# The second MLP's cosine with its argument in periods, its coefficients in two tiles, and a new order of instructions

## The chip, the cores and the metric

The kernel runs on one core of one Trainium2 chip. The metric is the device time of one execution in microseconds (us). The kernel before took 601.26 us, the median of three runs (601.25 to 602.89).

## The reference

The program computes an attention with a local window and block summaries, and behind it two MLPs on the same 1536 tokens of 512 features. Cut to what matters:

```python
# attention: 2 batches, 8 heads, 768 positions, 64 features a head
k_sum = k.reshape(B, H, nb, 32, D).max(axis=3)      # one maximum and one mean per block of 32
v_sum = v.reshape(B, H, nb, 32, D).mean(axis=3)
scores_l = scale * q @ k.T   # kept where |i - j| < 16
scores_s = scale * q @ k_sum.T + log(32)
a = softmax(concat([scores_l, scores_s]))
x = a @ concat([v, v_sum])
# first MLP: 512 -> 2048 -> 512
h = x @ w_in
g = (a0 + a1*h + a2*h**2 + a3*h**3) / (1 + abs(b0)*abs(h) + abs(b1)*h**2 + 1e-6)
x = g @ w_out
# second MLP, same sizes
h = x @ w_in
out = (h * cos(h)) @ w_out
```

All is in float32, except that the weights of both MLPs arrive as 8-byte floats.

## The kernel before

*Attention* is worked off in twelve units of 128 rows (six a batch). For the first batch, four pairs of heads are loaded as two k tiles each (line 454) and transposed on TensorE into a tile `ktp` (line 463); a copy (lines 322 and 327, by ScalarE or VectorE) puts them where the scores read them, and a reduction on VectorE (line 471) takes the maximum of the key blocks. The first unit's q rows come in two loads (line 559), are transposed into `qtp` (line 432) and copied to `qT`. Score products (line 626) go into `sp`; VectorE adds the mask and takes a row minimum (line 656), ScalarE takes the exponential, the normalised rows (line 673 multiplies) are transposed, and products with v (line 734, VectorE or GpSimd having added rows for the v means before) give the unit's output. The v means themselves are products with a selection matrix into `vmp` (line 542).

*The MLPs* take the tokens in three tiles T of 512 and the 2048 inner features in 16 tiles f of 128, four to a group. One pair of an f and a T is a unit; there are 48 a layer (the very first tile is cut in halves). A unit has its first product into `h` (line 864; in layer two from f = 2 on, two units share seven smaller products, line 962), its activation on ScalarE, VectorE and GpSimd, a split of the result into two parts `gh` and `gl` (lines 775 and 777), and the second product, which sums into four tiles `acc` (line 1106). Each product of 32-bit numbers is three TensorE products of such parts. The weights are put together from their 8-byte words by three VectorE instructions a tile (lines 760, 764, 768) and split in the same way. At the end of a group the `acc` tiles are copied out (line 1132), and put back (a copy again) when the token tile comes up next. When layer one has summed over all f, the copy is made by `x_keep` (line 893) and split for layer two; in layer two's last group the copies feed the output's DMAs, and the last of all are made by `mlp_end`.

*The activation of layer two* (`ew2`, lines 1045 to 1070) finds h·cos h. ScalarE turns h/2π into a whole number K (line 1057), VectorE takes K·2π from h in two steps, as 6.28125·K and the rest (line 1061, twice a unit), ScalarE takes the absolute value (line 1064) and then the sine of π/2 minus it (line 1066), and VectorE multiplies by h (line 1069).

*The coefficients* a and b come by two small loads into one tile `co`; three ScalarE and four VectorE instructions (lines 383 to 398) work out √|b1|, a scale that layer one's activation needs.

*The order.* The program first collects its operations (`P.op`), each with the engines that can do it, and then issues them in the order of a table, `ORDER`, which holds for each operation its place and the engine that does it. The times that stand with the operations are those by which the table was planned; with a table given they decide nothing. SyncE issues nearly all loads in its part of the same order. An engine works off its own part in order and waits where a tile that it needs isn't ready or isn't free.

## Time and profile before

| | |
|---|---|
| runs, median of 3 | 601.26 us |
| profiled execution, span | 599.4 us |
| TensorE busy (products) | 585.9 us, 98% |
| TensorE busy (weight loads, which run beside the products) | 501.0 us, 84% |
| VectorE busy | 548.4 us, 92% |
| ScalarE busy | 434.1 us, 72% |
| GpSimd busy | 304.3 us, 51% |
| granted TensorE clock | 9 in all 40 slices, which is 90% of full speed or more |

The profile is of one execution. The page gives its span, from its first to its last instruction, and no other time of that execution. In rows of the trace PE stands for TensorE, PEld for its weight loads, DVE for VectorE, ACT for ScalarE, POOL for GpSimd and SP for SyncE; L463 is line 463 of the kernel; `acc<-gh,w` says that `acc` is written from `gh` and `w`. The releaser named beside idle time is what ended it.

### The profile page before, as it was taken

Reading aid. Unit: us, or ns where it says so; the run is one execution under the profiler, and the core shown is the slowest. Engines: PE = TensorE matmul, PEld = TensorE weight load, DVE = VectorE, ACT = ScalarE, POOL = GpSimd, SP = SyncE. Lnnn points to the kernel's source line nnn. Section 1 sums busy time; section 2 is a strip of 40 time slices with the busy share of each in tenths; the row PEclk is TensorE's granted clock in tenths of the full one; section 3 lists DMA queues with packets and bytes.
Section 4 is the critical chain, followed back from the end, with each engine's and each line's share of the span. In section 5 each row is a group of like instructions: output and inputs, shape, how many; then the busy total and the mean of one; then the engine's idle time right before and its main releaser. Section 6 shows DMA issues by size and latency. Waiting matters only on the chain.

```text
span 599.4 us, 10933 instructions
## 1 busy us (share of the span) xinstructions
PE 585.9 (98%) x3897; PEld 501.0 (84%) x3897; DVE 548.4 (92%) x1119; ACT 434.1 (72%) x954; POOL 304.3 (51%) x303
## 2 busy tenths in 40 slices
PE   8879999999999999999999999999999999999997
PEld 7568878888888888888888888888989989998996
DVE  4999999979999999998999999999999998887874
ACT  3989999877587756876789897766767566554653
POOL 5587975247537564557577542444355423732130
PEclk9999999999999999999999999999999999999999
DMA  9897874200321313311220112123322331100104
GB/s 264 218 258 192 204 209 120 75 0 2 106 71 37 106 36 105 106 52 56 70 71 1 36 36 71 37 71 104 109 71 70 106 108 36 35 1 1 53 1 158
DMA packets 68862, 51.85 MB, mean 87 GB/s; under 512 B 37304, under 2 KB 63160, under 8 KB 68808
## 3 DMA queue, kind: packets, MB, share of 16 engines
q1 hardware_dynamic: 68664, 51.03, 29.0%
q8 instruction: 30, 0.49, 0.3%
q14 instruction: 24, 0.20, 0.1%
q10 hardware_dynamic: 144, 0.13, 0.1%
HBM read 47.71 MB, written 3.15 MB: 85 GB/s over the span
## 4 chain that ended last, share of the span: by engine, by line
PE 87%; DVE 9%; ACT 2%; DMA 1%; issue 0%; POOL 0%; SPq 0%; POOLq 0%; DVEq 0%; ACTq 0%
PE acc L1106 43%; PE h L864 22%; PE h L962 18%; DVE sc L656 2%; DMA vw<-in_v_dram 1%; PE avp L734 1%; DVE f L764 1%; DVE f L768 1%; PE ptp L687 1%; PE sp L626 1%; PE warm L356 1%; PE ktp L463 1%; DVE f L760 1%; PE vmp L542 0%; DVE big L471 0%
## 5 line engine op out<-in xcount | busy, mean ns | idle before, releaser
L1106 PE MATMUL acc<-gh,w 128*128 128x512 f32 (+1 forms) x416 | 123.1, 378 | 0.0
L1106 PE MATMUL acc<-w,gh 128*128 128x512 f32 x382 | 119.3, 394 | 0.0
L864 PE MATMUL h<-xH,w 128*128 128x512 f32 (+1 forms) x320 | 99.1, 371 | 0.1
L777 POOL TENSOR_TENSOR gl<-te,gh 128x512 fp32r<-128x512 f32 (+1 forms) x48 | 62.7, 1307 | 67.2 <-ACT gh L322 33.5
L1106 PEld LDWEIGHTS acc<-gh,w 128*128 128x128 f32 x416 | 75.3, 188 | 14.9 <-issue 1.5
L1106 PE MATMUL acc<-gl,w 128*128 128x512 f32 (+1 forms) x208 | 77.6, 373 | 0.0
L1106 PEld LDWEIGHTS acc<-w,gh 128*128 128x128 f32 x382 | 66.7, 189 | 9.4
L1106 PE MATMUL acc<-w,gl 128*128 128x512 f32 x191 | 74.3, 389 | 0.0
L1023 POOL TENSOR_TENSOR tu<-tu,tf 128x512 f32<-128x512 f32 (+1 forms) x41 | 51.4, 1255 | 41.2 <-ACT tf L1015 40.9
L777 POOL TENSOR_TENSOR w<-f,w 128x512 fp32r<-128x512 f32 x39 | 54.4, 1397 | 29.5 <-ACT w L322 15.0
L864 PEld LDWEIGHTS h<-xH,w 128*128 128x128 f32 x320 | 58.5, 188 | 10.6 <-DVE big L495 0.3
L864 PE MATMUL h<-xL,w 128*128 128x512 f32 (+1 forms) x160 | 58.9, 368 | 0.0
L864 PE MATMUL h<-big,w 128*128 128x512 f32 x216 | 52.0, 389 | 0.0
L768 DVE SCALAR_TENSOR_TENSOR f<-raw,f 128x512 int32<-128x512 int32 x64 | 48.3, 759 | 0.3
L1013 ACT ACTIVATE tu<-h,co 128x512 f32<-128x512 f32 (+1 forms) x52 | 33.9, 652 | 19.3 <-PE h L864 18.2
L764 DVE SCALAR_TENSOR_TENSOR f<-raw,f 128x512 int32<-128x512 int32 x64 | 47.3, 745 | 0.6
L864 PEld LDWEIGHTS h<-big,w 128*128 128x128 f32 x216 | 40.6, 188 | 8.4
L1106 PEld LDWEIGHTS acc<-gl,w 128*128 128x128 f32 x208 | 39.1, 188 | 7.0
L1106 PEld LDWEIGHTS acc<-w,gl 128*128 128x128 f32 x191 | 35.9, 188 | 7.9
L1057 ACT ACTIVATE tu<-te 128x512 int32<-128x512 f32 x27 | 17.1, 632 | 32.5 <-DVE te L987 32.2
L324 POOL TENSOR_SCALAR w<-f 128x512 fp32r<-128x512 f32 x28 | 20.0, 715 | 39.8 <-DVE f L768 35.1
L1033 ACT ACTIVATE h<-tf 128x512 f32<-128x512 f32 (+1 forms) x52 | 29.6, 570 | 12.0 <-DVE te L1027 10.8
(222 smaller groups left out, 1530.9 us busy)
## 6 DMA issues: line engine op xcount, KB each, us to landing
raw<-in_moe_w_in_dram SPq DMA_DIRECT2D x32, 512.0 KB, 4.6
raw<-in_moe_w_out_dram SPq DMA_DIRECT2D x32, 512.0 KB, 3.4
vw<-in_v_dram SPq DMA_DIRECT2D x24, 192.0 KB, 3.5
qk<-in_q_dram SPq DMA_DIRECT2D x10, 256.0 KB, 5.3
out_dram<-part SPq DMA_DIRECT2D x8, 256.0 KB, 2.8
part<-in_k_dram SPq DMA_DIRECT2D x8, 192.0 KB, 4.8
big<-in_v_dram SPq DMA_DIRECT2D x3, 512.0 KB, 6.7
qk<-in_k_dram SPq DMA_DIRECT2D x6, 256.0 KB, 5.4
```

The lines of the kernel that those rows point to most:

```text
L324: nc.gpsimd.tensor_scalar(out=o, in0=i, scalar1=1.0, scalar2=1.0, op0=ALU.mult, op1=ALU.mult)
L656: lambda e, pr=pr, hh=hh, sv=sv, sp=sp: nc.vector.tensor_tensor_reduce(out=sv()[:, pr, :], in0=sp.t[:, pr, :], in1=m.t, op0=ALU.add, op1=A ...
L764: lambda e: nc.vector.scalar_tensor_tensor(out=ft.t.bitcast(I32), in0=lohi()[1], scalar=-0x40000000, in1=ft.t.bitcast(I32), op0=ALU.bitwis ...
L768: lambda e: nc.vector.scalar_tensor_tensor(out=ft.t.bitcast(I32), in0=lohi()[0], scalar=29, in1=ft.t.bitcast(I32), op0=ALU.logical_shift_r ...
L777: lambda e: E[e].tensor_tensor(out=lo(), in0=x(), in1=hi().bitcast(F32), op=ALU.subtract),
L864: nc.tensor.matmul(out=h.t[:, 0:n], lhsT=lt, rhs=rt[:, kk, cs], start=(k0 == 0 and i == 0), stop=(k0 == 2 and i == 5))
L962: nc.tensor.matmul(out=bank.t[:, c], lhsT=lt, rhs=rt, start=start and i == 0, stop=stop and i == 5, skip_group_check=True)
L1013: lambda e: nc.scalar.activation(out=U(), in_=H(), func=ACTF.Square, scale=b1s))
L1023: lambda e: E[e].tensor_tensor(out=U(), in0=U(), in1=Z(), op=ALU.add))
L1033: lambda e: nc.scalar.activation(out=H(), in_=Z(), func=ACTF.Exp, scale=-1.0))
L1057: lambda e: nc.scalar.activation(out=K().bitcast(I32), in_=S_(), func=ACTF.Identity, scale=1.0 / (2.0 * math.pi)))
L1106: nc.tensor.matmul(out=dst, lhsT=lt, rhs=rt, start=(un.start and not have and i == 0), stop=(un.stop and i == 2), skip_group_check=have)
```

## The change

1. *The cosine.* From the output of layer one on, values are kept in a unit in which 0.875 (`PER`) is one period of the cosine: `x_keep` multiplies by 0.875/2π where it copied, and the output copies multiply by 2π/0.875. K is then h/0.875 + 0.25 as a whole number, and h − 0.875·K is one step, as 0.875·K needs few bits. The sine is taken of 2π/0.875 times this plus π/2, without an absolute value. Each of the 48 units of layer two loses one VectorE and one ScalarE instruction; 12 copies at the end of layer one and 13 at the output become scaled copies (`cps`).
2. *The coefficients.* a stays in `co`, b and what is made from it get a tile of their own, `cb`.
3. *The order.* The table is new (2944 operations instead of 3040). The planning times beside the operations are new too.

```diff
+PER = 0.875
+TURN = PER / (2.0 * math.pi)
 ORDER = (
-    "c-rk)ON?g6RsQOA-*w;jf4}<g{`)o4-P7Zq=^1+-9?wi>?7=wWB#vccTP8ROa%>aJ1|csTD`5dy#8QX>i%1qqK!CD{;t"
...
-MM = 0.2275
-SPT = 1.2
+MM = 0.2267
+SPT = 0.98
...
+    def cps(e, o, i, x):
+        if e == "A":
+            nc.scalar.activation(out=o, in_=i, func=ACTF.Identity, scale=x)
+        else:
+            nc.vector.tensor_scalar(out=o, in0=i, scalar1=x, scalar2=None, op0=ALU.mult)
...
-    co_r = fixed([128, 12], F32, "co")
-    co = co_r.t
+    co_r = fixed([128, 4], F32, "co")
+    cb_r = fixed([128, 5], F32, "cb")
+    co, cb = co_r.t, cb_r.t
...
-    b0, b1s = co[:, 4:5], co[:, 8:9]
+    b0, b1s = cb[:, 0:1], cb[:, 3:4]
...
-        P.op([("S", 0.1)], [], [co_r], lambda e: nc.sync.dma_start(out=co[:, 4:6], in_=moe_b.partition_broadcast(128)))
+        P.op([("S", 0.1)], [], [cb_r], lambda e: nc.sync.dma_start(out=cb[:, 0:2], in_=moe_b.partition_broadcast(128)))
-        P.op([("A", 0.2)], [], [co_r],
-             lambda e: nc.scalar.activation(out=co[:, 7:8], in_=co[:, 5:6], func=ACTF.Abs))
+        P.op([("A", 0.2)], [], [cb_r],
+             lambda e: nc.scalar.activation(out=cb[:, 2:3], in_=cb[:, 1:2], func=ACTF.Abs))
...
@@ x_keep
-        P.op([("A", act(512, True)), ("V", dve(512))], [ac], [rx[d]], lambda e: cp(e, x()[:, d], ac.t))
+        P.op([("A", act(512, True)), ("V", dve(512))], [ac], [rx[d]],
+             lambda e: cps(e, x()[:, d], ac.t, TURN))
@@ ew2
              lambda e: nc.scalar.activation(out=K().bitcast(I32), in_=S_(), func=ACTF.Identity,
-                                            scale=1.0 / (2.0 * math.pi)))
-        for c, x in ((C1, S_), (C2, H)):
-            P.op([("V", dve2(512) if x is S_ else dve(512))], [tu] + s2, hb,
-                 lambda e, c=c, x=x: nc.vector.scalar_tensor_tensor(
-                     out=H(), in0=K().bitcast(I32), scalar=-c, in1=x(), op0=ALU.mult, op1=ALU.add))
-        P.op([("A", act(512, True))], [], hb,
-             lambda e: nc.scalar.activation(out=H(), in_=H(), func=ACTF.Abs))
+                                            scale=1.0 / PER, bias=0.25))
+        P.op([("V", dve2(512) if un.s is not None else dve(512))], [tu] + s2, hb,
+             lambda e: nc.vector.scalar_tensor_tensor(
+                 out=H(), in0=K().bitcast(I32), scalar=-PER, in1=S_() if un.s is not None else H(),
+                 op0=ALU.mult, op1=ALU.add))
         P.op([("A", act(512, True))], [], hb + [table],
-             lambda e: nc.scalar.activation(out=H(), in_=H(), func=ACTF.Sin, scale=-1.0,
+             lambda e: nc.scalar.activation(out=H(), in_=H(), func=ACTF.Sin, scale=2.0 * math.pi / PER,
                                             bias=math.pi / 2))
@@ mlp_o
-                 lambda e, ac=ac, sl=sl: cp(e, sl(), ac.t))
+                 lambda e, ac=ac, sl=sl, last=un.last: (cps(e, sl(), ac.t, 1.0 / TURN) if last
+                                                        else cp(e, sl(), ac.t)))
@@ mlp_end
-            P.op([(e0, 0.3)], [ac], [res[x]], lambda e, c=c, sl=sl: cp(e, sl(), ac.t[:, c]))
+            P.op([(e0, 0.3)], [ac], [res[x]],
+                 lambda e, c=c, sl=sl: cps(e, sl(), ac.t[:, c], 1.0 / TURN))
```

What the new table moves is seen in the order in which each engine gets its instructions. Lines of the changed kernel stand six or seven further down than those of before. The first place is the opening of SyncE's queue, where `part` is the tile of the k and q loads, `big` that of v, and x2 says that a row stands for two instructions. Before:

```order
L454 DMA part<-in_k_dram 128x2x192 x2
L559 DMA part<-in_q_dram 128x4x128
L454 DMA part<-in_k_dram 128x2x192
L559 DMA part<-in_q_dram 128x4x128
L454 DMA part<-in_k_dram 128x2x192 x5
L507 DMA big<-in_v_dram 128x8x128 x3
```

After:

```order
L387 DMA cb<-in_moe_b_dram 128x2
L460 DMA part<-in_k_dram 128x2x192 x8
L565 DMA part<-in_q_dram 128x4x128 x2
L513 DMA big<-in_v_dram 128x8x128 x3
L421 DMA raw<-in_moe_w_in_dram 128x4x128
L421 DMA qk<-in_q_dram 128x8x64 x2
```

The load of b, which stood behind the opening, is first; the q loads, which stood between k loads, follow all eight of these.

The same opening on TensorE, where one k tile is six instructions of the `ktp` row, and one q load's transposition eight of the `qtp` row. Before:

```order
L356 MATMUL warm<-ident 128x128 x8
L463 MATMUL ktp<-ident,part 64x128 x12
L432 MATMUL qtp<-ident,part 64x64 x16
L463 MATMUL ktp<-ident,part 64x128 x30
L432 MATMUL qtp<-ident,part 64x64 x8
L626 MATMUL sp_290<-room,qT_214 64x120
L626 MATMUL sp_292<-room,qT_214 64x120
```

After:

```order
L362 MATMUL warm<-ident 128x128 x8
L469 MATMUL ktp<-ident,part 64x128 x48
L438 MATMUL qtp<-ident,part 64x64 x16
L632 MATMUL sp_303<-room,qT_290 64x120
L632 MATMUL sp_305<-room,qT_290 64x120
```

Two k tiles and both parts of the first q loads came ahead of five more k tiles and of the first score product; now all eight k tiles come first, then the q tiles.

The third place is VectorE's end, where the last two units of layer two are made (their h is in `h` and `te` or `tu`, `gl` is the low part that the last products read) and the last output copies stand (`room<-acc`). Before:

```order
L1061 SCALAR_TENSOR_TENSOR h<-tu,te 128x512
L1061 SCALAR_TENSOR_TENSOR h<-tu,h 128x512
L327 COPY acc_6848<-room 128x512
L327 COPY acc_6862<-room 128x512
L1069 TENSOR_TENSOR te<-te,h 128x512
L1061 SCALAR_TENSOR_TENSOR h<-tu 128x512
L327 CAST gh<-te 128x512
L1061 SCALAR_TENSOR_TENSOR h<-tu,h 128x512
L777 TENSOR_TENSOR gl<-te,gh 128x512
L1069 TENSOR_TENSOR tu<-tu,h 128x512
L327 CAST gh<-tu 128x512
L777 TENSOR_TENSOR gl<-tu,gh 128x512
```

After:

```order
L994 TENSOR_TENSOR te<-h,te 128x512
L332 COPY acc_6755<-room 128x512
L991 TENSOR_TENSOR tu<-h,tu 128x256
L1067 SCALAR_TENSOR_TENSOR h<-tu,te 128x512
L332 COPY tu<-h 128x256
L1074 TENSOR_TENSOR te<-te,h 128x512
L1067 SCALAR_TENSOR_TENSOR h<-tu 128x512
L783 TENSOR_TENSOR gl<-te,gh 128x512
L1074 TENSOR_TENSOR tu<-tu,h 128x512
L783 TENSOR_TENSOR gl<-tu,gh 128x512
```

One subtraction a unit is gone, and one copy back into `acc` stands between, where there were two. On TensorE 13 groups of three products stood between the last first-layer product and the first group that reads the last `gl`; now there are 8.

## Rows read from the trace of the kernel before

**Rows 1.** The head of the page: span, and busy time of each engine

```profile
span 599.4 us, 10933 instructions
...
PE 585.9 (98%) x3897; PEld 501.0 (84%) x3897; DVE 548.4 (92%) x1119; ACT 434.1 (72%) x954; POOL 304.3 (51%) x303
```

**Rows 2.** Busy us of PE, PEld, DVE, ACT, POOL; clock, DMA share, GB/s

```profile
0.00:20.00 20.00, 16.85 (x244) 13.66 (x244) 11.09 (x45) 9.28 (x35) 11.25 (x39) 1.00 0.94 262
20.00:40.00 20.00, 15.92 (x223) 12.07 (x222) 19.77 (x78) 19.33 (x75) 12.95 (x14) 1.00 0.87 218
40.00:60.00 20.00, 18.31 (x234) 16.43 (x235) 20.00 (x74) 18.97 (x67) 15.25 (x19) 1.00 0.81 219
...
420.00:440.00 20.00, 20.00 (x130) 18.16 (x129) 19.78 (x35) 15.08 (x32) 7.87 (x8) 1.00 0.41 127
```

**Rows 3.** TensorE in order of time: start, us, instruction, [idle before]

```profile
7.39 0.68 PE L432 MATMUL qtp<-ident,part 64*64 64x64 f32 x16
...
9.28 3.58 PE L463 MATMUL ktp<-ident,part 128*64 128x128 f32 x60
...
45.81 1.15 PE L734 MATMUL avp<-pt,vw 120*64 120x64 f32 x32
...
64.05 0.66 PE L489 MATMUL ktp<-ident,qk 128*128 128x128 f32 x4
...
73.53 1.02 PE L542 MATMUL vmp<-raw,vsel 128*24 128x512 f32 x2 [0.60 <-DVE mn L656]
...
94.77 1.44 PE L734 MATMUL avp<-pt,vw 120*64 120x64 f32 x32
...
591.96 0.62 PE L1106 MATMUL acc<-w,gh 128*128 128x512 f32 x2
```

**Rows 4.** The chain that ended last: start, us, what

```profile
14.71 1.44 DVE big L514
...
63.01 0.40 DVE te L1027
...
87.47 7.66 DMA vw<-in_v_dram
```

**Rows 5.** SyncE's queue in order of time, opening and end

```profile
0.81 0.94 SPq L454 DMA_DIRECT2D part<-in_k_dram  x2
...
3.36 2.56 SPq L454 DMA_DIRECT2D part<-in_k_dram  x5
...
593.45 2.86 SPq L1136 DMA_DIRECT2D out_dram<-room  x3
596.40 0.38 SPq L1159 DMA_DIRECT2D out_dram<-room  x1
```

**Rows 6.** DMA issues: line, count, KB each, us to landing

```profile
part<-in_k_dram SPq DMA_DIRECT2D x8, 192.0 KB, 4.8
...
co<-in_moe_b_dram SPq DMA_DIRECT2D x1, 1.0 KB, 8.1
```

**Rows 7.** VectorE in order of time, opening and end

```profile
14.44 0.27 DVE L656 CUSTOM_DVE_ANT_0 sc<-sp,room 128x120 f32<-128x120 f32 x1
...
590.58 0.69 DVE L777 TENSOR_TENSOR gl<-tu,gh 128x512 fp32r<-128x512 f32 x1
...
595.70 0.42 DVE L327 COPY room<-acc 128x256 f32<-128x256 f32 x1 [1.49 <-PE acc L1150]
```

**Rows 8.** Instructions by line and form: busy us, mean ns, idle before

```profile
L471 DVE TENSOR_REDUCE big<-ktp 128x12 f32<-128x384 f32 x8 | 4.1, 547 | 0.3 <-ACT big L322 0.3
...
L673 DVE TENSOR_TENSOR sc<-sc,su 128x480 f32<-128x480 f32 x1 | 0.7, 657 | 0.0
...
L322 ACT COPY big<-ktp 128x384 f32<-128x384 f32 x4 | 1.9, 480 | 6.6 <-PE ktp L463 6.6
...
L1061 DVE SCALAR_TENSOR_TENSOR h<-tu,h 128x512 f32<-128x512 int32 x47 | 32.5, 692 | 1.1
...
L1064 ACT ACTIVATE h<-h 128x512 f32<-128x512 f32 x47 | 27.4, 582 | 8.8 <-DVE h L1061 8.3
```

More of the change, by code (lines that the diff above doesn't have):

```diff
@@ L22 @@
 QC = 1.0 + 1e-6
-C1 = 6.28125
-C2 = 2.0 * math.pi - 6.28125
+PER = 0.875
+TURN = PER / (2.0 * math.pi)
 LAT = {}
@@ L102 @@
[L102 to L104 removed]
+    "c-rk)S&wANRX%Y}#NGGId-LAR%B3oos;nhz?XI47S543K^x|36J&lbS7#onM#|SJe8_C$iCXbmxgFv!8GD5N}d;DfI5A$Lh3"
+    "1bTcPY4Mfd4OmB0um3Lh`4F|h(JO}R8&=F-FqWWoaOtz6Pe%nPQfGL@t%|tD2Ax0J-7$&hF|r4$LWaJ0kz}5?a1E`7M?tlcu"
+    "WXigb9AW+XcPkc`4v~)2$#FG%#wQ?lqnxsw!w;78H|_g0xfT<YZkyB_9-i;9~`UfIaM~(o+b(1(7`bO?QO{uIrF@7>M_QT$r"
@@ new lines @@
+    "UPY&I@L1EhY_bRmE^{)!Vt4|DgS10My?^C9-{g99hd3&#)sQd}r;sSZB#sz7i)_A|fou7K^G?d|Iq7x3Y~I$SK^#&gesxIUd"
+    "8P7jVxrbjn!?484GYk&XEo!h|_=C|f=EEXSL(4UWaeD?G!mz$GouYBn7>G<doj9z|o^y2yNxep$!;OO{x?`NNNp#O6U>iPWR"
+    "FFT9H`MH!YKfd<-OJ#Xhjz6*`?_J(2yJdIyQva!bzuRywX0y&k{q4i)R`2Ofb<wF#N*IDDir#UREmjxXK{ng&WLx!gDrk@lV"
+    "OS5AvAc|-`Ti&7Js#0P8bLQmQxQI$CS~czof}Q(EI2NT@XezT?jEFf_74IXzy7-KM^7&np9mK-?^dvNe6khD$wBBmnyyyP=!"
+    "FNP`#U@L02X&1t2quYZ>K@+xSvk5_@1P*Cr{o#E9zwtNcpZul>c$;21GM{O4OsS3jEpqXWp26VcJmC>rwHLLZ=8*<xy1JzAZ"
@@ L105 @@
+    "E{Xc<bj4YV0CEo)txwuQH%Zn<n_MT?K2gD#l%3R~5;=NkhTG>%!Y+Nh-UpX^hM46+EZEtA>~gH{)*Ej6Om18VCJlG--iik9g"
+    "rQmn(LR=TX%uMuRo!!=lFt(m5#_M~NfG5woE$F~0F-C~9;tBtl;S+@FP0!0f7*;WqP4O_shQ*Dk=*d|-7byc(#H}%r}2CcZR"
+    "6~~moK+5i7j#L0^yyH)`BeErF`C{FoR+U;jQ=2ubovr(Z{HCflj<&g)Ca&u%Ta#;tT6zm}{Gyh2VEc+awCUTry~-9{`ZQxnr"
+    "H?hzTpKRP{{Yi98YT"
 )
@@ new lines, in coefficients @@
+        P.op([("A", 0.2)], [], [cb_r],
+             lambda e: nc.scalar.activation(out=cb[:, 3:4], in_=cb[:, 3:4], func=ACTF.Ln))
+        P.op([("A", 0.2)], [], [cb_r],
+             lambda e: nc.scalar.activation(out=cb[:, 3:4], in_=cb[:, 3:4], func=ACTF.Exp, scale=0.5))
+        P.op([("V", 0.1)], [], [cb_r], lambda e: nc.vector.reciprocal(out=cb[:, 4:5], in_=cb[:, 3:4]))
+        P.op([("V", Shared(0.1))], [], [cb_r],
+             lambda e: nc.vector.scalar_tensor_tensor(out=cb[:, 4:5], in0=cb[:, 4:5], scalar=cb[:, 2:3],
+                                                      in1=cb[:, 3:4], op0=ALU.mult, op1=ALU.add))
@@ L398, in coefficients @@
+        P.op([("V", Shared(0.1))], [], [cb_r],
+             lambda e: nc.vector.tensor_scalar(out=cb[:, 3:4], in0=cb[:, 4:5], scalar1=0.5, scalar2=None,
                                                op0=ALU.mult))
@@ L737, in mm @@
                             rhs=pts[hh].t[0:KW, pr, c0:c0 + 64], start=True, stop=True)
-        P.op([("T", 1.1)], pts + [vw[x] for vw in vw2 for x in "mw"], [op], mm)
+        P.op([("T", 1.08)], pts + [vw[x] for vw in vw2 for x in "mw"], [op], mm)
         T, c = divmod(128 * u, TT)
@@ L966, in prod @@
             reads = list(wr[:2]) + xo[0] + xo[1] + ([hx["b"]] if wn == "S1" else [])
-            P.op([("T", 6 * 0.12)], reads, [bank[half]] + ([hx["b"]] if wn == "11" else []), mm)
+            P.op([("T", 6 * 0.1185)], reads, [bank[half]] + ([hx["b"]] if wn == "11" else []), mm)
             P.now += 6 * 0.12
```

130 lines of the change are left out of this document (54 added, 76 removed).

## The prediction

> **What bounds the kernel now.** I read the page first [rows 1], then the busy times in stretches of 20 us [rows 2], then TensorE in order of time and the chain of waits where these show a loss [rows 3, 4], then the queue of loads and VectorE behind it [rows 5 to 7], and last the prices of single instructions [rows 8].
>
> The page has TensorE at 98% and VectorE at 92% of a span of 599.4 us. That is an average, and the stretches take it apart. In layer two (420 to 440 us) TensorE is busy for all of 20.00 us, at a granted clock of 1.00 as in the other stretches; in the first three it is busy for 16.85, 15.92 and 18.31 [rows 2]. These three lose 8.9 of the 13.5 us that TensorE loses over the span, so most of its loss lies where attention is worked off. Layer two, in which the removed work stands, has no loss to give back.
>
> In the opening the chain of waits runs over VectorE: from the v addition at 14.71 us to 63.41 us it names hardly anything else, then ScalarE, and from 73.5 us on TensorE [rows 4]. VectorE is busy for 19.77 and 20.00 us of 20 from 20 to 60 us [rows 2]. Until there, time is the moment of VectorE's first score block plus the work that VectorE has in front of what TensorE waits for. Later TensorE itself is the chain, with two losses: 0.60 us before the v mean of the second batch, until VectorE has read score blocks, and a product with v that takes 1.44 us where another takes 1.15, behind a load that holds the chain for 7.66 us [rows 3, 4].
>
> **The change, part by part.** *Cosine.* Each of 48 units loses one VectorE instruction (692 ns) and one ScalarE instruction (582 ns) [rows 8]: 33.2 and 27.9 us of engine time. All of it lies beside a TensorE that is busy without a gap, so I count 0. Its other bound is the 33.2 us of the third rival. The 25 scaled copies stand in place of plain ones of the same size, 12 where a token tile changes layer and 13 at the output. I count 0 for them too, under the same cover; without it, if each cost ScalarE's 0.1 us more and TensorE waited at the 12 changes, 1.2 us.
>
> The Trainium skill (Perfetto Trace Analysis, Identifying the Most-Contended Engine) says that matmul busy time is no measure of TensorE's headroom, that the busy share of its weight loads is, and that the engine with the highest occupancy is to be relieved. By that VectorE at 92% stands above weight loads at 84% [rows 1], and the 33.2 us would come off the span, to about 566. In the stretch at 420 us, though, TensorE has no idle time at all, and my sum goes by the stretch; the rule is the third rival.
>
> *The opening.* On SyncE's queue the load of b now comes first, then all eight k loads, then both first q loads, which stood third and fifth. On TensorE all eight k tiles are transposed in one piece. Before, two tiles were done at 7.39 us, then a q transposition and a wait came, and five tiles took 3.58 us from 9.28 [rows 3], 0.72 each. Now six follow at once: 7.39 + 6 x 0.72 = 11.7 us. Are the data there? Five k loads take 2.56 us to issue, 0.51 each, and land 4.8 us after issue [rows 5, 6]. With one issue more ahead, the eighth goes out at 0.81 + 8 x 0.51 = 4.9 us and lands near 9.7, before TensorE takes it at 11.0; the q loads land near 10.2 and 10.7. Then come one or two q transpositions (0.68 us each [rows 3]), a copy (0.42 for one of that size [rows 7]) and a score product (some 0.3): VectorE's first score block at 13.1 to 13.8 us, against 14.44 [rows 7]. I take 13.2, since the first unit's products need only the first of the two copies to start: 1.2 us, less 0.2 for a later wait of VectorE for the second unit's q: -1.0. Bounds: -0.2, if the load of b, which took 8.1 us to land in traffic [rows 6], holds up ScalarE, whose first instruction now reads it; -1.5, if copies and products overlap.
>
> *VectorE's work up to the last k transposition*, where VectorE is furthest behind TensorE. TensorE has the same 77 steps in front of it in both orders. VectorE has 154 instructions there in the old order and 150 in the new, 141 and 136 of them from the first score block on. Of these, gone are two k reductions (547 ns), the four coefficient instructions, which now lie in the opening, a v-mean copy and four small sums; come are two softmax multiplications (657 ns, POOL's before), two q copies and a window copy [rows 8]. Two multiplications for two reductions is +0.2, the copies +0.8, the coefficients, v-mean copy and sums -1.4 by their prices, and the rest evens out: -0.3 us (bounds 0 and -0.6).
>
> *After that* VectorE is some 1.5 us less behind, so the 0.60 us wait should go, and of the 0.29 us (1.44 less 1.15) I take half. That is -0.7. Against it stand four more changes between attention and layer products on TensorE (69 for 65), at an estimated 0.05 to 0.1 us each from matmul starts at such places: -0.5 (bounds 0 and -0.9). What is late next is TensorE itself.
>
> *The end.* Before, the last low part is written at 591.27 us, and the first matmuls of that unit start at 591.96 [rows 7, 3], 13 groups of three matmuls after the last first-layer product. Now it is 8 groups, 5 x 0.68 = 3.4 us earlier. The chain there has lost one instruction on each engine in two units, 2 x (0.69 + 0.58) = 2.5 us, and the acc copies that stood between are fewer; it just fits. The last output copy ends at 596.12 us but its DMA is issued at 596.40, since the queue is at work for another tile until 596.31 [rows 5, 7]; now the other tiles end before. Together -0.2 (bounds -0.3 and +1.0).
>
> Sum: -1.0 - 0.3 - 0.5 - 0.2 = -2.0 on the profiled execution's span of 599.4 us, 597.4. The runs' median of 601.26 is 1.9 above it (the page gives no other time of that execution); the same added gives **599.3 us**.
>
> **Rivals.** *The stage gives the opening back.* VectorE is full from 20 to 60 us, and ScalarE nearly so, 19.33 and 18.97 of 20; the DMA engines are busy for 0.81 to 0.94 of the first 60 us [rows 2]. Full engines that feed each other wait for each other the more the earlier they start, and loads come no faster. Then the end and half of the later gain are left: -0.4 us, 600.9. For it: the DMA shares. Against: neither engine is seen to wait for a load there.
>
> *ScalarE becomes the bound (slower).* Up to the last k transposition, at 64.05 us [rows 3], ScalarE has 138 instructions instead of 128, mainly three more k copies, a v-mean copy, sums and a cast: 2.9 us more by their prices. From 20 to 60 us it has 0.67 + 1.03 us free [rows 2], too little; the rest must come from the opening, where it waited 6.6 us for k tiles [rows 8]. If that doesn't shrink, 2.9 less the 1.0 won there is 1.9 us late, and the later gains go with it: 603.2. It decides from the point where ScalarE's busy time in the first 20 us stays under 11 us (9.28 now).
>
> *VectorE bounds layer two as well*: -33 us and 566, by the place and price above. Against: 20.00 of 20 us.
>
> *More than forecast.* If the contention that made one v addition last 1.44 us (another subtraction of its size takes 0.69 [rows 7]) goes too, and the later waits go in full, -4.5 us, 596.8.
>
> **How the numbers follow.** A measurement of this kernel tells about 0.3%, 1.8 us, from no change, so the borders are 599.5 and 603.1. Forecast (597.8 to 600.5): 0.50, six tenths of it below 599.5. Given back: 0.20. ScalarE: 0.16, half of it past 603.1, and of the other half 0.05 more, where the 1.2 us of the scaled copies come on top. More than forecast: 0.12. VectorE in layer two: 0.02. Faster is 0.30 + 0.12 + 0.02 and a tenth of the second case, 0.46; slower 0.13; no change 0.41. The range of 597.0 to 602.6 leaves out the third rival, half of the fourth and the far part of ScalarE's; the forecast's own is 597.8 to 600.5.
>
> **What would show it.** Right: VectorE's first score block near 13.2 us; the last k transposition near 62.8; no wait before the v mean; TensorE without idle time from 130 us on; VectorE and ScalarE less busy in layer two by some 33 and 28 us while the span shrinks by only 2; the last DMA issued within 0.6 us of the last matmul. Wrong: ScalarE in the chain between 20 and 60 us, its first copy after 8 us (b late), a gap on TensorE after 130 us, or a span shorter by ten or more.

## The result, and the profile after

The changed kernel takes 605.32 us, the median of four runs (604.38 to 607.15), and the kernel before 601.25 beside it: a ratio of 1.0071, 95% interval 1.0051 to 1.0090. It is slower by 4.1 us where 599.3 was forecast, and outside the range.

The head of the page after, to be held against [rows 1]:

```profile
span 603.1 us, 10820 instructions
...
PE 587.9 (97%) x3897; PEld 503.0 (83%) x3897; DVE 527.6 (87%) x1064; ACT 404.6 (67%) x904; POOL 313.0 (52%) x312
```

The removed work is gone: VectorE is busy for 20.8 us less, ScalarE for 29.5 us less. TensorE has the same 3897 matmuls and is busy for 2.0 us more. That it needs longer for the same work is the first sign of what was not foreseen. The span, 3.7 us longer, is TensorE's busy time, longer by 2.0, and its idle time, longer by 1.7 (15.2 us for 13.5). What is added to the idle time stands ahead of 130 us (length, then as in [rows 2]; before, then after):

```profile
0.00:130.00 130.00, 120.31 (x1433) 99.02 (x1434) 113.99 (x396) 107.38 (x357) 79.77 (x111) 1.00 0.67 178
0.00:130.00 130.00, 118.65 (x1418) 97.98 (x1419) 110.67 (x387) 108.27 (x359) 76.55 (x108) 0.99 0.68 178
```

By 130 us TensorE has been idle for 11.35 us, where it was 9.69; behind that it is idle for 3.8 us in both.

The stretches of [rows 2], after (length, busy us of PE, PEld, DVE, ACT and POOL, granted clock, DMA share, GB/s):

```profile
0.00:20.00 20.00, 16.01 (x241) 13.94 (x242) 9.07 (x41) 10.59 (x40) 11.15 (x41) 1.00 0.91 260
20.00:40.00 20.00, 16.91 (x194) 12.76 (x192) 18.03 (x68) 17.63 (x61) 7.89 (x7) 0.91 0.89 224
40.00:60.00 20.00, 16.66 (x218) 14.40 (x218) 19.49 (x73) 19.33 (x70) 15.59 (x18) 1.00 0.61 161
...
420.00:440.00 20.00, 20.00 (x122) 17.86 (x122) 16.09 (x27) 9.59 (x22) 8.75 (x9) 1.00 0.31 97
```

Layer two is as full as before, 20.00 of 20 us. The loss is in attention: 16.01 us where TensorE was busy for 16.85, 16.66 where it was 18.31; and from 20 to 40 us, where it is busy for longer (16.91 for 15.92), the mean granted clock was 0.91 where it was 1.00. In steps of 2 us the same view says where, after:

```profile
32.00:34.00 2.00, 0.52 (x2) 0.32 (x3) 2.00 (x6) 1.97 (x8) 0.46 (x1) 1.00 1.10 312
34.00:36.00 2.00, 2.00 (x13) 2.00 (x14) 2.00 (x12) 1.11 (x4) 1.28 (x1) 0.66 1.09 244
36.00:38.00 2.00, 2.00 (x10) 1.77 (x9) 1.00 (x3) 1.61 (x5) 0.10 (x1) 0.50 0.83 191
38.00:40.00 2.00, 1.88 (x16) 1.64 (x15) 1.97 (x5) 1.88 (x8) 0.64 (x1) 0.98 0.75 231
```

and before, in the thinnest piece of the same stretch:

```profile
38.00:40.00 2.00, 1.02 (x18) 0.72 (x14) 2.00 (x7) 2.00 (x9) 2.00 (x3) 1.00 0.97 240
```

After a piece with 0.52 us of work in 2.00 TensorE's clock falls from 1.00 to 0.50, from the higher to the lower of its two levels (2.4 and 1.2 GHz), and is back near 39 us. Against full speed that is 0.34 x 2 + 0.50 x 2 + 0.02 x 2 = 1.7 us, nearly all of the 2.0 by which TensorE is busy for longer. Before, 1.02 us of work in 2.00 went on at 1.00.

TensorE after in order of time (start, us, instruction, idle before it and what ended it), the rows that answer to [rows 3] and all waits of the opening:

```profile
11.67 0.68 PE L438 MATMUL qtp<-ident,part 64*64 64x64 f32 x16
12.86 0.62 PE L438 MATMUL qtp<-ident,part 64*64 64x64 f32 x13 [0.51 <-ACT qT L327]
...
14.01 0.72 PE L632 MATMUL sp<-room,qT 64*64 64x120 f32 x8 [0.26 <-ACT qT L327]
15.12 0.44 PE L632 MATMUL sp<-room,qT 64*64 64x120 f32 x8 [0.39 <-DVE mn L662]
...
17.10 0.64 PE L632 MATMUL sp<-room,qT 64*64 64x120 f32 x16 [0.31 <-DVE qT L332]
18.23 0.64 PE L632 MATMUL sp<-room,qT 64*64 64x120 f32 x10 [0.50 <-DVE mn L662]
19.47 0.43 PE L632 MATMUL sp<-room,qT 64*64 64x120 f32 x6 [0.60 <-DVE mn L662]
...
30.38 1.39 PE L740 MATMUL avp<-pt,vw 120*64 120x64 f32 x32
32.60 0.38 PE L870 MATMUL h<-xH,w 128*128 128x256 f32 x1 [0.83 <-ACT xH L327]
33.87 0.38 PE L870 MATMUL h<-xL,w 128*128 128x256 f32 x1 [0.88 <-DVE xL L751]
...
35.77 1.05 PE L587 MATMUL qtp<-ident,qk 128*128 128x128 f32 x4
...
45.85 0.66 PE L495 MATMUL ktp<-ident,qk 128*128 128x128 f32 x4 [1.22 <-ACT qT L327]
...
68.00 0.60 PE L495 MATMUL ktp<-ident,qk 128*128 128x128 f32 x4
...
76.53 1.04 PE L548 MATMUL vmp<-raw,vsel 128*24 128x512 f32 x2
...
599.14 0.50 PE L1156 MATMUL acc<-w,gh 128*128 128x256 f32 x2 [0.47 <-ACT room L321]
```

Six waits in the opening make up 2.57 us, and four of them end with VectorE, three of these in the middle of a unit's 32 score products, after VectorE has read a block of the same unit (`mn`: 15.12, 18.23 and 19.47). Behind the second unit's products with v (30.38) TensorE waits 0.83 and 0.88 us for both parts of x. At 35.77, at the lower clock, a q transposition takes 1.05 us that took 0.66 before (29.36 below). Its longest wait between 7 and 130 us, 1.22 us ahead of 45.85, is for a copy by ScalarE. The wait before the v mean [rows 3] is gone (76.53 has none). A new one of 0.47 us stands where three matmuls are left.

Before, TensorE's two waits from 7 to 21 us, and the place behind the second unit's products with v:

```profile
8.66 0.68 PE L432 MATMUL qtp<-ident,part 64*64 64x64 f32 x16 [0.59 <-ACT qT L322]
...
17.49 0.88 PE L626 MATMUL sp<-room,qT 64*64 64x120 f32 x16 [1.03 <-ACT room L322]
...
27.74 0.33 PE L734 MATMUL avp<-pt,vw 120*64 120x64 f32 x2 [0.43 <-ACT pt L322]
...
29.36 0.66 PE L581 MATMUL qtp<-ident,qk 128*128 128x128 f32 x4
30.74 1.05 PE L626 MATMUL sp<-room,qT 64*64 64x120 f32 x32 [0.72 <-ACT qT L322]
31.72 0.38 PE L864 MATMUL h<-xH,w 128*128 128x256 f32 x1
31.94 0.28 PE L864 MATMUL h<-xL,w 128*128 128x256 f32 x1
```

Neither wait of the opening ended with VectorE. A q transposition and a unit's score products (29.36 and 30.74) covered the splitting of x, and neither part of it was waited for, though the scores waited 0.72 us for their q. VectorE after, beside [rows 7]:

```profile
13.95 0.28 DVE L662 CUSTOM_DVE_ANT_0 sc<-sp,room 128x120 f32<-128x120 f32 x1 [0.77 <-PE sp L632]
...
14.77 0.28 DVE L662 CUSTOM_DVE_ANT_0 sc<-sp,room 128x120 f32<-128x120 f32 x1 [0.53 <-PE sp L632]
...
31.66 1.35 DVE L770 SCALAR_TENSOR_TENSOR f<-raw,f 128x512 int32<-128x512 int32 x1
```

The first score block comes at 13.95 us, 0.49 earlier than before, not 1.2. Then VectorE waits for TensorE again (0.53), while TensorE waits for VectorE: the two take turns.

The chain that ended last, of which [rows 4] has pieces of before, ran over VectorE from 18 to 63 us with hardly a break. Now it is TensorE's from 19.90 to 23.73 us, then ScalarE's for some 5.3 us, and VectorE's again from 29.63 us on, with a break at the slow products (33.87 to 36.84). The first and the last piece of ScalarE's:

```profile
23.74 0.59 ACT qT L327
...
29.11 0.49 ACT xH L327
```

SyncE's queue, beside [rows 5]:

```profile
1.24 4.00 SPq L460 DMA_DIRECT2D part<-in_k_dram  x8
...
600.32 0.33 SPq L1166 DMA_DIRECT2D out_dram<-room  x1
```

The loads go out as forecast, and TensorE waits for none of them in the opening.

What makes the two engines take turns can't be seen in the order of either. In the built program a wait is set for a whole tile: four blocks of a unit's scores lie in each of two `sp` tiles, and where the table places VectorE's reading of one block ahead of the product for the next, that product waits for the reading, though it writes another part of the tile. The new table places them so. Five of the first unit's 16 score products on TensorE in the changed kernel, the fifth to the ninth, with what each row waits for:

```
MATMUL sp0<-room,qT 64x120 [waits Activation]
MATMUL sp1<-room,qT 64x120 [waits DVE]
MATMUL sp0<-room,qT 64x120
MATMUL sp1<-room,qT 64x120
MATMUL sp0<-room,qT 64x120 [waits DVE]
```

The planner's times track the pieces apart, so the plan did not see these waits.

### The profile page after: what moved, and what is told of

Same layout as the page of the kernel before. It is cut to its first block, busy times and chain, and to the rows that moved or that the text cites. A ratio compares the mean times of both kernels' runs of the same rounds, so it can differ in the third digit from the quotient of the medians.

```text
span 603.1 us, 10820 instructions
## 1 busy us (share of the span) xinstructions
PE 587.9 (97%) x3897; PEld 503.0 (83%) x3897; DVE 527.6 (87%) x1064; ACT 404.6 (67%) x904; POOL 313.0 (52%) x312
## 4 chain that ended last, share of the span: by engine, by line
PE 91%; DVE 6%; ACT 2%; DMA 1%; issue 1%; POOL 0%; POOLq 0%; DVEq 0%
PE acc L1111 43%; PE h L870 23%; PE h L969 17%; PE avp L740 1%; PE sp L632 1%; PE ptp L693 1%; DVE sc L662 1%; PE ktp L469 1%; PE qtp L587 1%; DMA qk<-in_q_dram 1%; PE warm L362 1%; DVE f L770 1%; DVE f L774 1%; DVE xL L751 0%; PE vmp L523 0%
## 5 line engine op out<-in xcount | busy, mean ns | idle before, releaser
L870 PE MATMUL h<-xH,w 128*128 128x512 f32 (+1 forms) x320 | 100.4, 374 | 0.8 <-ACT xH L327 0.8
L783 POOL TENSOR_TENSOR gl<-te,gh 128x512 fp32r<-128x512 f32 (+1 forms) x54 | 71.4, 1322 | 37.6 <-ACT gh L327 24.7
L783 POOL TENSOR_TENSOR w<-f,w 128x512 fp32r<-128x512 f32 x41 | 55.8, 1363 | 45.9 <-ACT w L327 32.1
L870 PEld LDWEIGHTS h<-xH,w 128*128 128x128 f32 x320 | 59.1, 190 | 11.7 <-ACT xH L327 1.0
L1020 ACT ACTIVATE tu<-h,cb 128x512 f32<-128x512 f32 (+1 forms) x52 | 33.9, 654 | 21.1 <-PE h L870 17.6
L1071 ACT ACTIVATE h<-h 128x512 f32<-128x512 f32 x48 | 27.6, 584 | 20.1 <-DVE h L1067 20.1
L666 ACT ACTIVATE sc<-sc,mn 128x120 f32<-128x120 f32 x96 | 37.2, 390 | 3.1 <-DVE mn L662 2.9
L1042 DVE SCALAR_TENSOR_TENSOR tu<-tu,h 128x512 f32<-128x512 f32 (+1 forms) x52 | 33.2, 640 | 5.8 <-ACT h L1040 4.9
```

The lines of the kernel that those rows point to most:

```text
L666: lambda e, pr=pr, hh=hh, sv=sv: nc.scalar.activation(out=sv()[:, pr, :], in_=sv()[:, pr, :], func=ACTF.Exp, scale=-1.0, bias=mn.t[:, hh, ...
L783: lambda e: E[e].tensor_tensor(out=lo(), in0=x(), in1=hi().bitcast(F32), op=ALU.subtract),
L870: nc.tensor.matmul(out=h.t[:, 0:n], lhsT=lt, rhs=rt[:, kk, cs], start=(k0 == 0 and i == 0), stop=(k0 == 2 and i == 5))
L1020: lambda e: nc.scalar.activation(out=U(), in_=H(), func=ACTF.Square, scale=b1s))
L1042: lambda e: nc.vector.scalar_tensor_tensor(out=U(), in0=U(), scalar=QC, in1=H(), op0=ALU.add, op1=ALU.mult))
L1071: lambda e: nc.scalar.activation(out=H(), in_=H(), func=ACTF.Sin, scale=2.0 * math.pi / PER, bias=math.pi / 2))
```

## The experiments

Each ran beside the kernel before on the same chip. The changed kernel was not run again beside them, so it is compared by the ratios to the kernel before. "At full clock" is the median of those runs whose mean granted clock over the whole execution was 0.998 or more; n is how many of the runs that are.

| edit | us | ratio to before [95%] | at full clock (n) |
|---|---|---|---|
| changed kernel (first measurement) | 605.32 | 1.0071 [1.0051, 1.0090] | (0 of 4) |
| e1 cosine alone, old order | 601.17 | 1.0003 [0.9992, 1.0013] | 601.14 (11 of 12) |
| e2 old order to 70 us | 602.92 | 1.0030 [1.0020, 1.0039] | 602.92 (11 of 12) |
| e3 all products of a unit first | 603.08 | 1.0036 [1.0021, 1.0051] | 602.54 (6 of 12) |
| e4 matmuls repeated in a wait | 606.57 | 1.0086 [1.0065, 1.0107] | (0 of 6) |
| e5 old order to 25 us | 605.42 | 1.0066 [1.0042, 1.0090] | 603.14 (1 of 6) |
| e6 e2, end taken apart | 603.07 | 1.0028 [1.0012, 1.0045] | 602.71 (9 of 12) |
| e7 old order to 130 us | 609.47 | 1.0135 [1.0117, 1.0153] | (0 of 5) |
| e8 products first, end apart | 602.94 | 1.0029 [1.0015, 1.0043] | 602.31 (8 of 12) |
| e9 low part of x earlier | 605.64 | 1.0075 [1.0057, 1.0093] | (0 of 6) |
| e10 e8 with e9 | 602.23 | 1.0022 [1.0012, 1.0033] | 602.16 (9 of 12) |
| e11 e8, low part of x later | 604.27 | 1.0047 [1.0033, 1.0062] | 602.92 (2 of 6) |
| e12 e1, end adjacent | 601.66 | 1.0009 [1.0000, 1.0018] | 601.47 (10 of 11) |
| e13 e1, wait before v mean gone | 600.95 | 0.9994 [0.9980, 1.0009] | 600.78 (10 of 12) |
| e14 e10, copies before conversion | 602.32 | 1.0017 [1.0002, 1.0032] | 601.60 (7 of 12) |
| e15 e11, wait filled with matmuls | 603.32 | 1.0035 [1.0021, 1.0049] | 602.85 (8 of 11) |
| e16 e8's products, end as it was | 602.88 | 1.0031 [1.0015, 1.0046] | 602.40 (8 of 12) |

The kernel before had medians of 601.01, 601.40, 600.91 and 601.02 in the four groups (e1 to e4, e5 to e8, e9 to e12, e13 to e16). Of its runs 28 of 29, 18 of 23, 22 of 23 and 28 of 35 were at full clock, so a share of full-clock runs is to be held against that of its own group.

**e1, the cosine alone.** The changed code with the table of before, less the 96 operations that are gone.

```diff
 the table ORDER of the kernel before, in it 48 times each:
-SCALAR_TENSOR_TENSOR h<-tu,h 128x512
-ACTIVATE h<-h 128x512
```

> The changed kernel with the order of before (without the 96 instructions that the cosine no longer has): the cosine, the scaled copies and the two coefficient tiles alone. In the changed kernel's trace the unit output products (avp) are late by 1.9 us for the first unit, 3.3 for the third and 4.1 for the sixth, and nothing is lost behind 73 us, so the theory that the whole loss stands in the order of the opening expects 601.3 us (600.5 to 602.0). The rival that the scaled copies or the lighter cosine cost time expects 602.5 or more.

The ratio is 1.0003. Its page:

```profile
span 599.1 us, 10856 instructions
...
PE 585.6 (98%) x3897; PEld 500.7 (84%) x3897; DVE 525.9 (88%) x1071; ACT 408.2 (68%) x906; POOL 303.6 (51%) x303
```

22.5 us of VectorE and 25.9 of ScalarE [rows 1] bought nothing that can be told from the scaled copies and the second tile, which are in the same run: together they change the time by no more than the interval, -0.5 to +0.8 us. The 4.1 us are the new order's, within that.

**e2 and e5, old order up to a time.** The first 560 (e2) or 175 (e5) operations of the old table, then the new one; e7 the same with 1000.

```diff
-the new table
+the first 560 operations of e1's table, then the others in the new table's order
```

> The changed kernel with the order of before up to about 70 us and the new order behind it. Theory (the loss lies in the first 70 us): 601.0 us, 600.0 to 601.8. Rival (the new order loses its time later, in the changes between attention and layer products or at the end): 604 or more. My forecast that the later part of the new order gains 0.7 would make it 600.5.

> The changed kernel with the order of before for the opening alone (until about 25 us) and the new order behind it. Theory (the opening of the new order makes TensorE's work thin and late; the clock's fall follows from it): granted clock mean 0.998 or more as with the old order, and about the 602.9 of the run with the old order to 70 us (602.3 to 603.5). Rival (the fall of the clock comes from the new order between 25 and 70 us, where TensorE waits 1.7 us for xH and xL): mean clock 0.995 and 604 or more.

> The changed kernel with the order of before through attention (to about 130 us) and the new order behind it. Theory (of the 1.9 us that old order to 70 us and new order behind lost, 0.9 lie at 70 to 130 us and 0.5 to 0.75 at the end): 601.9. Rival (the layers in the new order lose it): 602.9. If the lighter cosine and the new order of the layers gain anything: under 601.2.

With the old order to about 70 us (e2) it is 602.92: 1.8 us of the loss are left, by the ratio, with 11 of 12 runs at full clock, where the theory had 601.0 and the rival 604. That does not place 1.8 us of the changed kernel's loss behind 70 us, since joining two orders makes waits of its own: from 60 to 100 us TensorE is idle for 0.77 us before, 0.93 in the changed kernel and 1.65 in e2 (profiled executions). With the old order to 25 us (e5) it is 605.42, as in the changed kernel, and in five of six runs the mean clock is 0.997 or less. Either the opening's waits are not the cause by themselves, or the seam at 25 us made idle time of its own (TensorE is busy for 15.13 us from 20 to 40 us, in the profiled execution); this run can't tell which. e7 made a hole: TensorE waited 4.79 us at 163.49 us, and the granted clock was 0.66 from 160 to 170. It tells nothing about its question (601.9 or 602.9 was expected).

**e3 and e16, products before readings.** e3 puts all score products of the first two units ahead of their score blocks in the table; e16 does so for the first three quarters of the first unit's products and all of the second's. In e16 TensorE, VectorE, GpSimd and SyncE have row for row the order of the changed kernel, and ScalarE has one copy moved behind one exponential. What differs is which row waits, here on TensorE:

```diff
 MATMUL sp0<-room,qT 64x120 [waits Activation]
-MATMUL sp1<-room,qT 64x120 [waits DVE]
+MATMUL sp1<-room,qT 64x120
 MATMUL sp0<-room,qT 64x120
 MATMUL sp1<-room,qT 64x120
-MATMUL sp0<-room,qT 64x120 [waits DVE]
+MATMUL sp0<-room,qT 64x120
```

> The changed kernel with the score products of each of the first two units ahead of the VectorE score blocks that read the same two tiles, instead of alternating with them in the program's order; each engine's own instructions stay nearly in place (VectorE reads one block two places later). Theory (a product that writes one part of a tile is made to wait until VectorE has read another part of it, which the table doesn't reckon with): VectorE's six waits of 0.2 to 0.5 us between 13 and 20 us go, the first unit's output product starts 1 to 2 us earlier, 603.6 us. Rival (TensorE's clock, which falls to 1.2 GHz at 34.5 to 38 us, is the whole loss): no change, 605.3, unless the clock no longer falls.

> The changed kernel with the score products of the first two units mended and nothing else. By the runs so far (605.3 as it is; 602.94 with the end apart as well; the end worth 0.5 to 0.75): 603.5, with a mean clock of 0.998 or more. Rival (the end apart did most of it): 604.7 and the clock as low as in the changed kernel.

Both give back about half or more, 603.08 and 602.88 (603.6 and 603.5 were expected). In e3 the readings had to wait for the last quarter, whose q stood behind other transpositions, and VectorE began late:

```profile
16.28 0.28 DVE L669 CUSTOM_DVE_ANT_0 sc<-sp,room 128x120 f32<-128x120 f32 x1 [2.79 <-POOL big L527]
```

e16 leaves that quarter where it was. Its score products in the opening from the first unit's last quarter on, and the second unit's products with v:

```profile
16.01 0.64 PE L644 MATMUL sp<-room,qT 64*64 64x120 f32 x16 [0.68 <-ACT room L339]
17.08 0.85 PE L644 MATMUL sp<-room,qT 64*64 64x120 f32 x24 [0.42 <-ACT room L339]
...
29.07 1.39 PE L752 MATMUL avp<-pt,vw 120*64 120x64 f32 x32
```

None of the opening's waits ends with VectorE's `mn` any more, and the second unit's products with v start at 29.07 instead of 30.38. With the same rows on the engines, but for that one copy, the 2.4 us between e16 and the changed kernel (by the ratios) are the price of the waits, and of what they do to the clock: 8 of 12 runs are at full clock, where none of four was.

**e8, e6 and e12, the end.** In the new order the two halves of the last product stand next to each other, and the second half's product waits for ScalarE's copy of the first half out of the same `acc` tile (the 0.47 us above). e6 and e8 put another group of three products between them, as before; e12 does the reverse to e1.

```diff
 MATMUL acc<-w,gl 128x512
-MATMUL acc<-w,gh 128x512 x2
-MATMUL acc<-w,gl 128x512
 MATMUL acc<-w,gh 128x256 x2
 MATMUL acc<-w,gl 128x256
+MATMUL acc<-w,gh 128x512 x2
+MATMUL acc<-w,gl 128x512
 MATMUL acc<-w,gh 128x256 x2
```

> The kernel with the old order to 70 us (602.92), and at the end another group of three products between the two halves of the last one, as before. In the new order the second half waits 0.47 us for ScalarE's copy of the first half out of the same tile. Theory: the last product ends 0.5 to 0.75 us earlier and the time is 602.3. Rival (the output's queue sets the end anyway): 602.9.

> The changed kernel with two places of its order mended: in each of the first two units those score products that need not wait stand ahead of the first score block (three of four in the first unit, all in the second), and the last product's halves stand apart. Against the run with all products first (603.1), VectorE starts 1 us earlier and ScalarE's sixteen exponentials, which set the first two units' output products there, follow without a wait: theory 600.7 (600.0 to 601.8) with a mean clock of 0.998 or more. Rival (the opening isn't set by these waits): 602.4, the 603.1 less the end.

> The changed kernel with the order of before (601.17), and at the end the two halves of the last product one behind the other, as in the new order, instead of another group between them. Theory: the second half waits 0.47 us for the copy of the first out of the same tile, and the last product ends 0.5 to 0.75 us later: 601.7. Rival (the output's queue hides it): 601.2.

e12 makes the wait in the old order, and is slower than the kernel before beside it by 0.75 us by the medians and 0.5 by the ratio (interval 0.0 to 1.1); against e1, from which it differs by this alone, it is 0.4 by the ratios, and the intervals overlap:

```profile
595.82 0.50 PE L1165 MATMUL acc<-w,gh 128*128 128x256 f32 x2 [0.61 <-ACT room L330]
```

In e6 the wait is gone from the trace and the time is that of e2 within the noise (602.3 was expected), as is e8's against e16's. e8 was expected at 600.7, or at 602.4 by its rival, and is at 602.94. The wait is half a microsecond on TensorE, but no run shows that much time for it clear of noise, and the traces suggest why: what follows TensorE's last product is shorter with the wait (from 599.76 to 603.1 us in the changed kernel, from 597.20 to 601.0 in e2, from 596.44 to 599.9 in e12) than without it (from 595.59 to 599.4 before, from 596.11 to 600.4 in e6, from 595.26 to 599.1 in e1): 3.3 to 3.8 us for 3.8 to 4.3.

**e4, e9, e10: is it the idle time at 32 us that lets the clock fall?** e4 repeats the first layer product eight times in the wait at 33 us, with no use of what it gives; e9 fills that place with the next q transposition and makes x's low part before a conversion of weights; e10 is e8 with the same.

```diff
+for _ in range(8 if un is units[0] and k0 == 0 and i == 0 else 0):
+    nc.tensor.matmul(out=h.t[:, 0:n], lhsT=lt, rhs=rt[:, kk, cs], start=True, stop=True)
```

```diff
 TensorE
+MATMUL qtp<-ident,qk 128x128 x4
 MATMUL h<-xH,w 128x256
...
-MATMUL qtp<-ident,qk 128x128 x4
 VectorE
-SCALAR_TENSOR_TENSOR f<-raw,f 128x512
 ISA sc,mn<-sp,room 128x120
...
 TENSOR_TENSOR xL<-avp,xH 128x4x128
+SCALAR_TENSOR_TENSOR f<-raw,f 128x512
```

> The changed kernel with the first layer product repeated eight times in the gap of 0.88 us in which TensorE waits for the low part of x (33.0 to 33.9 us). Theory (the idle stretch of 31.8 to 34 us is what lets the granted clock fall to 1.2 GHz from 34.5 to 38 us, where 3.5 us of TensorE's work take twice as long): clock 1.00 there and 603.9 us (-1.1 to -1.7). Rival (VectorE is the chain there and hides the slow products): clock 1.00 and no change, 605.3. If the clock falls all the same, the repeated products don't count as filling.

> The changed kernel; only around 32 us: the q transposition of the fourth unit stands ahead of the first layer-one product instead of behind it, and VectorE does five score blocks and the low part of x ahead of a weight conversion. Theory (TensorE's idle stretch of 31.8 to 33.9 us, where it waits for xH and xL, is what the clock falls behind in most executions): TensorE idle there for 0.6 us instead of 1.7, mean granted clock 0.998 or more, 603.0 us (602.4 to 603.8). Rival (the clock falls from the thin opening at 12 to 20 us or elsewhere): clock still 0.995, 605.

> The same change at 32 us in the kernel with the score products mended and the end apart (602.94, mean clock 0.999). Theory: the executions with a low clock go, and the median falls to that of the executions at full clock, 602.2; faster than before (under 601.2) only if the 0.7 us lost at 70 to 130 us went too, which nothing here touches. Rival: no change, 602.9.

The theory that this place is the cause is not borne out: e4 was expected at 603.9 and e9 at 603.0, with the clock up. In e4's profiled execution the clock is at 1.00 there and falls earlier and later:

```profile
14.00:20.00 6.00, 4.90 (x79) 3.85 (x81) 2.93 (x22) 3.98 (x20) 2.56 (x3) 0.58 0.99 260
...
32.00:44.00 12.00, 10.25 (x148) 8.78 (x145) 11.57 (x41) 11.59 (x40) 6.37 (x8) 1.00 0.99 239
44.00:52.00 8.00, 6.45 (x55) 5.46 (x53) 7.51 (x34) 6.54 (x25) 6.83 (x8) 0.60 0.53 142
```

In e9 the waits at 32 us shrink and the clock falls ten us later:

```profile
32.00:40.00 8.00, 6.04 (x67) 4.92 (x65) 7.66 (x19) 7.72 (x27) 3.40 (x4) 1.00 0.92 238
40.00:44.00 4.00, 3.12 (x42) 2.40 (x37) 3.68 (x14) 3.73 (x16) 3.66 (x6) 0.67 0.92 254
```

Neither gained. With the opening mended as well (e10) it is 602.23, as its theory had it; but against e8 that is 0.4 us by the ratios with intervals that overlap, and 3 of its 12 runs are still below full clock.

**e11 and e15: idle time and the clock, the other way round.** e11 is e8 with x's low part three VectorE instructions later, so that TensorE waits 1.83 us for it; e15 is e11 with the first layer product repeated ten times in that wait.

```diff
-TENSOR_TENSOR xL<-avp,xH 128x4x128
 RECIPROCAL su<-su 128x4
 SCALAR_TENSOR_TENSOR f<-raw,f 128x512
 ISA sc,mn<-sp,room 128x120
+TENSOR_TENSOR xL<-avp,xH 128x4x128
```

> The kernel with the score products mended and the end apart (602.94, mean clock 0.999), with the low part of x three VectorE instructions later, so that TensorE waits for it some 1.0 us longer (0.34 us there). Theory (the idle stretch makes the clock fall): mean clock 0.996 or less and 604.5 or more, over 1.5 us for a wait of 1.0. Rival (only the wait itself counts): clock 0.999, at most 603.9.

> The kernel with the low part of x late (604.27, mean clock 0.997, TensorE waiting 1.83 us at 32 us), with the first product of layer one repeated ten times in that wait. The products that count start as late as without. Theory (idle time lets the clock fall): mean clock 0.999 and 602.9, the time of that kernel's executions at full clock. Rival (the clock falls for something else in the opening): 0.997 and 604.3.

The longer wait costs 1.1 us against e8 by the ratios, and 2 of 6 runs are at full clock instead of 8 of 12. Filled, it is 603.32, with 8 of 11 at full clock. The twelfth execution of e15, the profiled one, took 831.53 us at a mean granted clock of 0.654 and is in none of these numbers. Its trace has the clock at 0.65 from 6 us on, ahead of the repeated products (36 us), and to the end, though TensorE is busy for all of the time from 80 to 800 us: in that execution no idle time explains the clock, and the filled wait has no trace at the usual speed. At full clock the two are alike (602.92 and 602.85), so the 0.7 us between them by the ratios would be the clock's; their intervals overlap, though, as do those of e8 and e11, and this is a support and no proof. It is no rule for a single execution either. e11's profiled execution had this stretch and kept its clock:

```profile
30.00:36.00 6.00, 3.23 (x34) 2.65 (x29) 3.94 (x18) 4.54 (x17) 2.86 (x2) 1.00 0.89 250
```

**e13, the wait before the v mean.** e1 with one VectorE instruction of the first MLP's activation behind the eight score blocks that the product waits for.

```diff
-TENSOR_SCALAR te<-h,co 128x256
 ISA sc,mn<-sp,room 128x120
...
+TENSOR_SCALAR te<-h,co 128x256
```

> The changed kernel with the order of before, and one VectorE instruction (a first step of the layer-one activation, 0.53 us) moved behind the eight score blocks that TensorE's v mean waits for at 73.5 us. Theory: the wait of 0.60 us there falls to 0.1 and the time to 600.6 (601.17 without the move). Rival (TensorE then waits as long at a later place): 601.2.

```profile
73.50 1.02 PE L559 MATMUL vmp<-raw,vsel 128*24 128x512 f32 x2
74.45 1.35 PE L643 MATMUL sp<-room,qT 64*64 64x120 f32 x32
```

The 0.60 us wait [rows 3] is gone, but the product starts where it started before (73.53 us), and the score products behind it take 1.35 us: in this execution nothing was won. At 0.9994 [0.9980, 1.0009] it can't be told from the kernel before, nor can a gain of the expected 0.6 us be ruled out; no version was shown to be faster than the kernel before.

**e14, the wait at 86 us.** In e10 a conversion on VectorE stands ahead of the copy that TensorE waits for at 86 us; e14 puts the two copies first.

```diff
-SCALAR_TENSOR_TENSOR f<-raw,f 128x512
 COPY qT<-qtp 128x512
 COPY pt<-ptp 120x512
+SCALAR_TENSOR_TENSOR f<-raw,f 128x512
```

> The kernel of 602.23 us (score products mended, end apart, change at 32 us), and at 84 us two copies that TensorE waits for (qT and pt) ahead of a weight conversion of VectorE instead of behind it; the conversion lasts 1.82 us there, 0.66 elsewhere, beside a subtraction of GpSimd of 1.27 us. Theory: the wait of 0.51 us at 86 us goes, 601.7. Rival (it comes back later): 602.2.

The wait goes from the trace. By the median, 602.32, nothing is won; at full clock it is 601.60 for e10's 602.16, on seven and nine runs, which is a hint and not a proof (601.7 was the theory's, 602.2 the rival's).

## Why the prediction was wrong, point by point

*The cosine at nothing:* right (e1), though the busy time of VectorE and ScalarE fell by 22.5 and 25.9 us and not by 33 and 28. The third rival, by which VectorE's 33.2 us would come off the span, is refuted: e1 has VectorE at 88% instead of 92% and the same time. The rule of the Trainium skill that went with it (Perfetto Trace Analysis, Identifying the Most-Contended Engine), taken over the whole span, does not hold here.

*The opening, -1.0.* This is the step that failed. The k tiles ended as worked out, the next transposition starting at 11.67 us for 11.7, and no load was late. But the second q transposition waited 0.51 us for the copy of the first out of their one tile, and the first score block came at 13.95, not 13.2. More than that: the first score block was taken as the moment from which VectorE's work runs on without a break, and in the new order it does not: the chain leaves VectorE until 29.63 us, for TensorE and then for ScalarE. The products with readings between them wait for whole tiles (three of the opening's six waits, 1.49 of 2.57 us), and the second unit's products with v start 2.6 us late (30.38 for 27.74). The order that I had counted in instructions carried its waits in the places of the table, and I had not read them.

*VectorE's work, -0.3, and later waits, -0.5.* From 29.63 us on the chain is VectorE's again, but it starts late and its 0.3 us are lost in that. The last k transposition, forecast for 62.8, comes at 68.00, for 64.05 before [rows 3]. The wait before the v mean is gone, as forecast, but by luck: VectorE was to be less behind there, and it is TensorE that comes 3.0 us later (76.53 for 73.53). That the wait was worth 0.6 us is not shown either (e13).

*The end, -0.2.* It came out at nothing: the halves of the last product follow each other and the second waits 0.47 us, and what follows the last product is about as much shorter (3.3 us for 3.8). The last DMA is issued at 600.32, 0.56 us after the last matmul, as forecast, and TensorE has no other wait worth naming from 130 us on. I had seen that the acc copies moved, and not that the two halves had become neighbours in one tile.

*Not in the sum at all: the clock.* In [rows 2] it was 1.00 everywhere, so no price stood against thinning TensorE out. In the four runs of the changed kernel mean granted clock and time go together: 0.992 with 607.15 us, 0.994 with 605.76, 0.996 with 604.88, 0.997 with 604.38. That is 2.77 us for 0.005, 0.55 for each 0.001, and at 1.000 about 604.38 - 3 x 0.55 = 602.7 (a line through four runs, an estimate). So of the 4.1 us some 2.6 are the clock's and some 1.5 the order's at full clock. In the profiled execution, at 0.996, the parts are 1.7 us of clock between 34 and 40 us and 1.7 of idle time, all of it by 70 us; the end has no share. Mending only the waits on whole tiles (e16) gave back 2.4, by the clock mostly: at full clock e16 is at 602.4.

*The rivals.* "The stage gives the opening back" was nearest in kind, full engines that wait for each other, but it had 600.9 and its reason was DMA shares. "ScalarE becomes the bound" gave nearly the right time at its upper end by a mechanism that is half right. Its sign came: ScalarE's busy time in the first 20 us is 10.59, under its limit of 11, and ScalarE is in the chain between 20 and 60 us, which the prediction named as a sign of being wrong. But it was to be too full for its extra work, and it is not: it is busy for 17.63 and 19.33 us from 20 to 60, for 19.33 and 18.97 before. Why it is in the chain isn't shown: in e16, with the waits on whole tiles gone, the chain still runs over it, with short breaks, from 21.3 to 28.3 us, mostly copies and exponentials, and no run tested what that costs.

*What stays open.* What makes the clock fall in a given execution isn't settled. The place differs (34 us after, 14 and 44 in e4, 41 in e9), and filling one place moved it to another. That the waits on whole tiles make a fall likelier is shown by e16 (8 of 12 runs at full clock, for none of 16 in the changed kernel, e4 and e9, which keep these waits); that it is idle time on TensorE that does it is supported by e11 and e15, and against it stand e5 and the long execution of e15. The 1.2 us or so at full clock by which e10 is behind the kernel before was not taken apart further than e14. The wait of 1.22 us for ScalarE's copy of q (45.85 us after) stands in the traces of e10, e14 and e16 too, and no run took it away.

## What to carry to other kernels

Where a table or a planner sets the order, read which instructions wait, not only where they stand: two programs with the same rows on TensorE, VectorE, GpSimd and SyncE differed by 2.4 us. Put the products that fill one tile ahead of its first reader; giving the parts tiles of their own, which was not tried here, is another way. And when TensorE is the bound, an order that leaves it idle a little longer early on may pay again in its clock, so compare a few runs at equal mean clock before giving a median to the order.
